# Sliding-window attention beside a gated feed-forward: small vector operations on other engines, masked maxima in two instructions, and TensorE's blocks taken from two lanes

## The chip, the cores and the metric

The kernel runs on one core of one Trainium2 chip. The metric is device time in microseconds, the median of the runs shown. Lower is better.

## What is computed

Sequence length S = 2048, model width D = 512, 32 heads of width 16, window W = 256, feed-forward width F = 1792, all float32:

```python
xn = layernorm(x)
q, k, v = heads(xn @ wqkv)
scores = (q @ k.T) / 4                      # key within the last 256 tokens, else -1e9
s = (softmax(scores) @ v) @ wo
h = silu(xn @ w1) * (xn @ w3)
g = silu(h @ w2)
return x + s * g
```

## The kernel before

**Number format.** Each float32 operand of a large matmul is cut into a float16 high half and a float16 low half, after a scaling by a power of two, and three products (high by high, high by low, low by high) stand for one. So every weight tile passes through a chain: a scale that is worked out from sums of squares (`powers`, `measure`, `measure_down`, a dozen VectorE instructions on 1 to 6 columns), a scaled copy and a rounding on ScalarE (L319, L320), a subtraction in two halves on GpSimd (L316). During the first quarter of the tokens these cut weights are used straight away and stored to DRAM; later quarters load them back.

**Stages.** The tokens are worked in four tiles of 512, t = 0 to 3. Heads go in four groups g of eight, each group in two parts p, which makes 32 units (t, g, p). Beside the units run the projections (L550, L520), the gate and up matmuls of the feed-forward for 14 blocks f (`gate_up`, L937), the down projection (`down`, L987, for t = 0 and the end; `product`, L1040, with a seven-product scheme for halves after that) and the output projection (`total`, L1118).

**Attention.** `pass1` computes scores of a row of queries (L604) only to find each query's maximum. Two 512-column banks hold the scores, one per head r. For each bank one VectorE instruction adds a mask (`MW` or `M1`, 0 or -1e30) and takes the maximum (L616), followed by a read of the accumulator. At the end of a unit the maxima are scaled and cut into two float16 parts on VectorE (L621, L622, tile `NM`), turned by a small matmul (L631), copied out (L637) and sent by DMA to two extra rows of the queries, so that `pass2`'s score matmuls (L678) subtract them. `pass2` adds masks to some blocks (L685, VectorE), takes the exponential (L688, ScalarE) and multiplies by V (L706). Each V head has a 17th column of ones, whose sums are the softmax denominators; `normalise` inverts them (L743) and scales them by `sc["o"]` (L744). K's extra rows hold +4096 and the maxima go in with a minus sign.

**Tokens prepared beside.** For t = 1 to 3, `prepare` computes mean and variance (L422, L423), then a reciprocal square root by a bit trick and three Newton steps on [128, 4] tiles, all on VectorE (`rstd`, L427 to L437), centres the tokens (L440) and turns them through unused columns of score banks (`turn_beside`, L478), where VectorE writes the float16 high part (L487) and the rest (L488).

**Banks.** Dense matmuls (tile size 128x128) accumulate in two PSUM banks m0 and m1 in turn. Scores use two tiles s of two banks and one tile po. A down block in bank m1 is added to its SBUF sum by VectorE (L1007) before the next block may use m1.

**What sets the order.** TensorE executes in the order in which the program is written: `spread` distributes dense pieces between five batches of score matmuls per unit. For VectorE, ScalarE, GpSimd and the DMA queue on SyncE, `listed` plays the program through a cost model (`arrange`) and puts each engine's instructions in the order in which they are taken there, by latest start; three rounds, the best is kept.

Of the kernel before, what the change touches and what calls it, by code (L numbers as in the profile page):

```python
# [21 lines left out]
P = 128  # L22
# [26 lines left out]
TWO_ONES = struct.unpack("f", struct.pack("ee", ONE, ONE))[0]  # L49
# [44 lines left out]
def tile_block(ctx: ExitStack, tc: tile.TileContext, x, wqkv, wo, w1, w3, w2, out):  # L94
# [121 lines left out]

    MK = const.tile([P, 3, 2, 64], BF16, name="MK")
# [48 lines left out]
    def powers(sb, n, p2, inv, s=None):  # L266
# [16 lines left out]
        def rest():  # L283
            if s is None:
                nc.vector.tensor_scalar(al, ps, 2.08, 1e-30, op0=ALU.mult, op1=ALU.max)
            else:
                with urgent():
                    nc.vector.tensor_scalar(al, s[:, 0, WIN:WIN + n], 2.08, 1e-30, op0=ALU.mult, op1=ALU.max)
                    nc.vector.scalar_tensor_tensor(al, s[:, 1, WIN:WIN + n], 2.08, al, op0=ALU.mult, op1=ALU.add)

            nc.vector.tensor_scalar(al.bitcast(I32), al.bitcast(I32), 24, 23, op0=ALU.logical_shift_right,
                                    op1=ALU.logical_shift_left)
            nc.vector.tensor_scalar(p2, al, 2.0**63, None, op0=ALU.mult)
            nc.vector.reciprocal(inv, p2)
# [8 lines left out]

    def scaled(a, by, name):
        t = const.tile([P, 1], F32, name=name)
        nc.vector.tensor_scalar(t, a, by, None, op0=ALU.mult)
# [60 lines left out]
    def weights_qk(g):  # L367
# [19 lines left out]
        def cut(ks=(1, 0)):  # L387
# [12 lines left out]
            nc.vector.tensor_scalar(es, cell["p2"], cell["p2"], DH**-0.5 / QS**2, op0=ALU.mult, op1=ALU.mult)  # L400
# [9 lines left out]
    def prepare(t):  # L410
# [9 lines left out]
        def stats(b):  # L420
            st = lnpool.tile([P, nc.vector.BN_STATS_DIM], F32, name="st")
            nc.vector.bn_stats(st, xts[b])  # L422
            nc.vector.bn_aggr(mv[:, b, :], st)  # L423

# [42 lines left out]
        def turn_beside(b, n, s):  # L467
# [24 lines left out]
        return load, stats, rstd, centre, turn if t == 0 else turn_beside  # L492
# [95 lines left out]
    def pass1(t, g, p):  # L588
# [6 lines left out]
        def part(ii, a, beside):  # L595
# [17 lines left out]
            for r in range(2):  # L613
                junk = ppool.tile([P, D], BF16, name="junk", bufs=1)
                with urgent():
                    nc.vector.tensor_tensor_reduce(  # L616
                        out=junk[:, :n], in0=s[:, r, :n], in1=mask, scale=1.0,
                        scalar=NEG, op0=ALU.add, op1=ALU.max, accum_out=M[:, r, a, ii:ii + 1])
# [117 lines left out]
    def normalise(t, g):  # L736
# [33 lines left out]
    def load(t, f):  # L770
        if t:
            WF[t, f] = a, b = [take(F16) for _ in range(2)], None if halved(t, f) else take(F16)
            for k in range(2):
                nc.sync.dma_start(a[k], dW1[f, k])
            if b is not None:
                nc.sync.dma_start(b, dW2[f])
            return
        RAW[f] = raw = [take(F32) for _ in range(2)]
        for k, w in enumerate((w1, w3)):
            nc.sync.dma_start(raw[k].rearrange("p (c f) -> p c f", f=P),  # L780
                              w[:, f * P:(f + 1) * P].rearrange("(c p) f -> p c f", p=P))

    measured = set()

    def measure(f, apart=0):
# [10 lines left out]
        def rest(pp, pi):  # L796
            ff = slice(f, f + 2)
            nc.vector.tensor_scalar(pi, pi, WS, None, op0=ALU.mult)
            nc.vector.tensor_scalar(sg_scale[:, ff], pp[:, 0, :], 0.5 / (WS * XS), None, op0=ALU.mult)
            nc.vector.tensor_mul(p13[:, ff], pp[:, 0, :], pp[:, 1, :])  # L800
# [29 lines left out]
    def measure_down(k, f):  # L830
# [16 lines left out]
        def rest(p2):  # L847
            assert measured >= set(range(f0, f1))
            nc.vector.tensor_mul(p2, p2, p13[:, f0:f1])
            q = small.tile([P, 1], F32, name="q")  # L850
            nc.vector.tensor_reduce(q, p2, axis=AX.X, op=ALU.max)
            nc.vector.tensor_scalar(down_scale[:, k:k + 1], q, 1.0 / (HS * WS), None, op0=ALU.mult)
            nc.vector.reciprocal(q, q)
            sw = small.tile([P, 6], F32, name="sw2")
            nc.vector.tensor_scalar(sw[:, 0:n], p13[:, f0:f1], q, WS, op0=ALU.mult, op1=ALU.mult)
# [304 lines left out]
    def feed_forward():  # L1160
# [7 lines left out]
        for t in range(NT):  # L1168
            for f in range(FB):
# [12 lines left out]
                else:  # L1182
                    if f == 0:
                        pieces += [(0, lambda t=t, f=f: load(t, f)) for f in range(2)]
                    if f + 2 < FB:
                        pieces.append((0, lambda t=t, f=f + 2: load(t, f)))
                if f == FB - 4 and t + 2 < NT:
# [111 lines left out]
    for b in range(4):  # L1299
# [4 lines left out]
                         AF.Copy, scale=ONE)  # L1304
# [398 lines left out]
```

## Time and profile before

| | |
|---|---|
| time, median of 3 runs | 819.23 us (818.41 to 819.41) |
| the profiled execution, its own time | 821.13 us |
| span of the profiled execution | 819.3 us, mean granted TensorE clock 0.994 |
| TensorE busy | 797.9 us (97%) |
| VectorE, ScalarE, GpSimd busy | 639.2, 435.3, 358.7 us (78%, 53%, 44%) |
| DMA | 121.99 MB, mean 149 GB/s |

TensorE is the engine that the span is made of. The profile counts a matmul of 512 columns as busy for 0.38 us, to its modelled end, though the next one starts 0.22 us after it; so the 97% hides waits of up to some 0.16 us, and what a wait costs is read from the rows of the waits and the timeline. "Sparse" below means matmuls on tiles smaller than 128x128 (scores, V, turning), "dense" the others.

### The profile page before, as it was taken

Reading aid. Unit: us, or ns where it says so; the run is one execution under the profiler, and the core shown is the slowest. Engines: PE = TensorE matmul, PEld = TensorE weight load, DVE = VectorE, ACT = ScalarE, POOL = GpSimd, SP = SyncE. Lnnn points to the kernel's source line nnn. Section 1 sums busy time; section 2 is a strip of 40 time slices with the busy share of each in tenths; the row PEclk is TensorE's granted clock in tenths of the full one; section 3 lists DMA queues with packets and bytes.
Section 4 is the critical chain, followed back from the end, with each engine's and each line's share of the span. In section 5 each row is a group of like instructions: output and inputs, shape, how many; then the busy total and the mean of one; then the engine's idle time right before and its main releaser. Section 6 shows DMA issues by size and latency. Waiting matters only on the chain.

```text
span 819.3 us, 23768 instructions
## 1 busy us (share of the span) xinstructions
PE 797.9 (97%) x9088; PEld 415.8 (51%) x9088; DVE 639.2 (78%) x2044; ACT 435.3 (53%) x659; POOL 358.7 (44%) x556
## 2 busy tenths in 40 slices
PE   8999999699999999999999999999999999999998
PEld 4444444344544554454555555545555555545654
DVE  8898889977897777799778866777878787774535
ACT  6898799555636554443443455534443446544421
POOL 2247646672806433523341752514141456435252
PEclk9999999899999999999999999999999999999999
DMA  9996575268665334545364452426375543224521
GB/s 284 284 296 185 164 215 169 75 197 204 176 179 136 117 103 121 152 144 154 106 189 133 125 142 69 140 72 172 112 185 152 159 146 113 56 90 149 172 65 55
DMA packets 112835, 121.99 MB, mean 149 GB/s; under 512 B 18448, under 2 KB 77008, under 8 KB 112720
## 3 DMA queue, kind: packets, MB, share of 16 engines
q1 hardware_dynamic: 112432, 119.94, 51.2%
q8 instruction: 71, 1.16, 0.6%
q10 hardware_dynamic: 288, 0.52, 0.2%
q14 instruction: 44, 0.36, 0.1%
HBM read 83.76 MB, written 32.37 MB: 142 GB/s over the span
## 4 chain that ended last, share of the span: by engine, by line
PE 83%; DVE 12%; issue 2%; DMA 1%; ACT 1%; DVEq 0%; SPq 0%; ACTq 0%
PE m L937 32%; PE m L1040 9%; PE m L550 9%; PE po L706 8%; PE s L678 5%; PE m L1118 5%; PE m L520 5%; PE m L987 4%; DVE junk L616 3%; PE s L604 3%; DVE s L685 2%; PE po L604 2%; DVE st L422 1%; DMA qa<-dQ 1%; DVE slot L957 1%
## 5 line engine op out<-in xcount | busy, mean ns | idle before, releaser
L688 ACT ACTIVATE pt<-s,es 128x1024 f32<-128x1024 f32 x152 | 167.7, 1113 | 198.0 <-DVE s L685 193.3
L937 PE MATMUL m<-XH,slot 128*128 128x512 f16 x896 | 267.4, 380 | 1.0 <-DVE slot L952 0.8
L316 POOL TENSOR_TENSOR slot<-slot,slot 128x256 f16<-128x256 f32 (+1 forms) x222 | 148.6, 696 | 152.4 <-ACT slot L320 66.6
L937 PEld LDWEIGHTS <-slot 128*128 128x128 f16 x1344 | 124.5, 98 | 152.6 <-issue 12.3
L937 PE MATMUL m<-XL,slot 128*128 128x512 f16 x448 | 169.8, 379 | 0.0
L685 DVE TENSOR_TENSOR s<-s,MK 128x256 f32<-128x256 f32 (+2 forms) x280 | 120.7, 437 | 50.4 <-PE s L678 41.9
L616 DVE CUSTOM_DVE_ANT_0 junk<-s,MW 128x320 bf16<-128x320 f32 x276 | 134.5, 487 | 28.0 <-PE s L604 18.6
L906 POOL TENSOR_TENSOR slot<-slot,slot 128x256 f16<-128x256 f32 x133 | 87.9, 685 | 46.4 <-ACT slot L902 46.3
L1040 PE MATMUL m<-slot,slot 128*128 128x256 f16 x798 | 96.4, 276 | 2.0 <-DVE s L685 1.8
L616 DVE CUSTOM_DVE_ANT_0 junk<-po,MW 128x320 bf16<-128x320 f32 x172 | 84.0, 488 | 10.0
L1040 PEld LDWEIGHTS <-slot 128*128 128x128 f16 x798 | 76.9, 99 | 20.4 <-issue 4.5
L706 PE MATMUL po<-pt,V 64*32 64x320 f32 (+4 forms) x2880 | 78.2, 345 | 0.0
L706 PEld LDWEIGHTS po<-pt,V 64*32 64x32 f32 x2880 | 51.9, 106 | 23.8 <-PE s L604 4.0
L910 POOL TENSOR_TENSOR slot<-slot,slot 128x256 f32<-128x256 f32 x19 | 14.2, 747 | 102.8 <-DVE slot L957 96.5
L678 PE MATMUL s<-qa,KA 50*64 50x320 f16 (+3 forms) x1472 | 58.2, 259 | 1.0 <-ACT pt L688 1.0
L987 PE MATMUL m<-slot,slot 128*128 128x512 f16 x216 | 51.6, 386 | 7.0 <-DVE slot L1007 4.7
L952 DVE SCALAR_TENSOR_TENSOR slot<-slot,m 128x512 f32<-128x512 f32 x56 | 38.3, 683 | 24.0 <-ACT slot L948 23.8
L678 PEld LDWEIGHTS <-KA 50*64 50x64 f16 x1472 | 30.2, 105 | 50.9 <-issue 36.3
L716 ACT COPY os<-po 128x512 f32<-128x512 f32 x32 | 18.7, 585 | 70.2 <-PE po L706 70.2
L948 ACT ACTIVATE slot<-m,sgs 128x512 f32<-128x512 f32 x56 | 38.3, 684 | 32.2 <-PE m L937 31.3
L957 DVE SCALAR_TENSOR_TENSOR slot<-m,slot 128x512 f32<-128x512 f32 x56 | 38.5, 687 | 15.9 <-PE m L937 15.5
L604 PE MATMUL s<-KA,qa 48*64 48x320 f16 (+2 forms) x648 | 45.5, 295 | 1.9 <-DVE M L616 0.7
(170 smaller groups left out, 1137.1 us busy)
## 6 DMA issues: line engine op xcount, KB each, us to landing
slot<-dW SPq DMA_DIRECT2D x88, 256.0 KB
slot<-dR SPq DMA_DIRECT2D x56, 256.0 KB
slot<-in_B_w_dram SPq DMA_DIRECT2D x42, 256.0 KB
dW<-slot SPq DMA_DIRECT2D x32, 256.0 KB
slot<-in_A_x_dram SPq DMA_DIRECT2D x30, 256.0 KB
KA<-dK SPq DMA_DIRECT2D x24, 288.0 KB
dR<-slot SPq DMA_DIRECT2D x49, 128.0 KB
qa<-dQ SPq DMA_DIRECT2D x32, 192.0 KB
```

The costliest lines, as they stand in the source:

```text
L316: op(out[:, c], a[:, c], b[:, c])
L550: nc.tensor.matmul(cell["pp"], a[:, k, c, :], b[:, c, :], start=(c, i) == parts[0][0], stop=(c, i) == parts[-1][-1])
L604: nc.tensor.matmul(s[64 * c:64 * c + 64, r, :n], qa[rows, 2 * p + a, ii * P + 64 * c:ii * P + 64 * c + 64], ka[rows, 2 * p + a, e - n:e], ...
L616: nc.vector.tensor_tensor_reduce(out=junk[:, :n], in0=s[:, r, :n], in1=mask, scale=1.0, scalar=NEG, op0=ALU.add, op1=ALU.max, accum_out=M[ ...
L678: nc.tensor.matmul(s[64 * h:64 * h + 64, r, o:o + 64 * n], ka[rows, 2 * p + a, 64 * (m + 4):64 * (m + 5)], qa[rows, 2 * p + a, 64 * (m + k ...
L685: nc.vector.tensor_add(v, v, MK[:, kind, of:of + n, :].unsqueeze(1).to_broadcast([P, 2 * len(which), n, 64]))
L688: nc.scalar.activation(pt, s, AF.Exp, scale=es)
L706: nc.tensor.matmul(cell["po"][32 * i:32 * i + 32, h, 64 * (m + k):64 * (m + k + n)], V[64 * h:64 * h + 64, (4 * t + m // 2) % VB, hd * VW: ...
L906: nc.gpsimd.tensor_sub(made[:, D + c.start:D + c.stop], raw[:, c], made[:, c])
L937: nc.tensor.matmul(cell[k], w[:, (a * NC + c) * P:(a * NC + c + 1) * P], b[:, c, :], start=c == 0 and i == 0, stop=c == NC - 1 and i == 2)
L987: nc.tensor.matmul(ps, hh[:, a * TW + b * P:a * TW + (b + 1) * P], w[:, c * D:(c + 1) * D], start=f == f0 and i == 0, stop=f == f1 - 1 and ...
L1040: nc.tensor.matmul(ps[:, blk, :], l[:, a * D + q:a * D + q + 128], r[:, 256 * c:256 * c + 256], start=f == f0 and x == 0, stop=f == f1 - 2 ...
```

## The change

1. **Masked maxima.** For all rows but the first two of the sequence, the two mask-and-maximum instructions become one predicated copy over both banks, which puts columns 0 to 63 over columns 256 to 319 where the far mask `PM` is set, and one plain maximum over columns 64 to 319 of both banks. Nothing then masks columns that stand in the future by adding: a column inside the window takes their place, and the leading 64 columns are left out of the maximum.
2. **Small operations moved.** The two-part cut of the maxima goes to ScalarE (two instructions) and GpSimd (one). The scale chains of weights (`powers`, `measure`, `measure_down`, `scaled`, `es`, `us`) that run beside the units go to GpSimd but for their reads of PSUM, integer shifts, one maximum and one reciprocal; a reciprocal of a power of two becomes integer arithmetic. The reciprocal square root of t = 1 to 3 goes to GpSimd (`rstd_beside`, 15 instructions). The high part of turned tokens (L487) goes to ScalarE. The scaling L744 goes away: V's columns of ones hold the scale instead, written by one ScalarE instruction in place of ten GpSimd memsets. K's extra rows hold -4096.
3. **Two lanes.** TensorE's instructions are cut into blocks, dense ones of at most six matmuls and sparse ones by PSUM tile. The planner may take the head of the other lane when the next block is not ready within 300 ns, and the order it finds is kept for TensorE too.
4. **The cost model** of `arrange` has new figures, a delay for same-engine reads, a lock between GpSimd and some VectorE instructions, and four rounds.

```diff
+    def aside():
+        return nc.gpsimd if started else nc.vector
...
+            op = nc.vector if s is None else nc.gpsimd
...
+            op.tensor_scalar(p2, al, 2.0**63, None, op0=ALU.mult)
+            if s is None:
+                nc.vector.reciprocal(inv, p2)
+            else:
+                op.tensor_scalar(inv.bitcast(I32), p2.bitcast(I32), -1.0, float(254 << 23), op0=ALU.mult, op1=ALU.add)
...
+        def rstd_beside(b0, b1):
+            op = nc.gpsimd
+            ve = lnpool.tile([P, b1 - b0], F32, name="ve")
+            op.tensor_scalar(ve, mv[:, b0:b1, 1], 1e-5, None, op0=ALU.add)
...
+            for i in range(3):
+                op.tensor_mul(sq, r0, r0)
+                op.tensor_mul(sq, sq, ve)
+                op.tensor_scalar(sq, sq, -0.5, 1.5, op0=ALU.mult, op1=ALU.add)
+                op.tensor_mul(r0, r0, sq)
...
-                    nc.vector.tensor_copy(hi, pt)
+                    nc.scalar.copy(hi, pt)
                     nc.vector.tensor_sub(lo, pt, hi)
...
-            for r in range(2):
-                junk = ppool.tile([P, D], BF16, name="junk", bufs=1)
+            if i >= 2:
                 with urgent():
-                    nc.vector.tensor_tensor_reduce(
-                        out=junk[:, :n], in0=s[:, r, :n], in1=mask, scale=1.0,
-                        scalar=NEG, op0=ALU.add, op1=ALU.max, accum_out=M[:, r, a, ii:ii + 1])
+                    nc.vector.copy_predicated(s[:, :, 256:320], PM.unsqueeze(1).to_broadcast([P, 2, 64]), s[:, :, 0:64])
+                    nc.vector.tensor_reduce(M[:, :, a, ii:ii + 1], s[:, :, 64:320], axis=AX.X, op=ALU.max)
...
-                nc.vector.tensor_scalar(nm[:, 0, :], Mf, -1.0 / ONE, None, op0=ALU.mult)
-                nc.vector.scalar_tensor_tensor(nm[:, 1, :], Mf, -1.0 / ONE, nm[:, 0, :], op0=ALU.mult, op1=ALU.subtract)
+                nc.scalar.activation(Mf, Mf, AF.Copy, scale=1.0 / ONE)
+                nc.scalar.copy(nm[:, 0, :], Mf)
+                nc.gpsimd.tensor_sub(nm[:, 1, :], Mf, nm[:, 0, :])
...
-            nc.vector.tensor_scalar(dr, dr, sc["o"], None, op0=ALU.mult)
...
+PIECE, GAIN, LEADING, FOLLOW = 6, 300, 8000, 0.0
...
+            first = met[able[0]] if not open_[able[0]] else None
+            if len(able) > 1 and (first is None or first > f + GAIN):
+                o = able[1]
+                if not open_[o] and when_of[o] - when_of[able[0]] < LEADING and (
+                        first is None or max(f, met[o]) + GAIN < first):
+                    return max(f, met[o]), o
...
-    for e in engines[1:]:
+    for e in engines:
         for a, b in zip(best_order[e], best_order[e][1:]):
```

**How the orders differ.** Line numbers shift: L316 is L333 after, L604 L635, L616 L652, L646 (predicated copy) and L647 (maximum), L678 L715, L685 L722, L987 L1030, L1007 L1050, L488 L519, L440 L471.

VectorE, in the down projection of t = 0, group of blocks f = 4 to 9: bank m1 holds the sum `m_2573` (after: `m_2540`) of the first 128 tokens, and L1007 (after: L1050) empties it. Before, it stands behind the whole reciprocal square root of the next tokens:

```order
L435 SCALAR_TENSOR_TENSOR sq<-sq,ve 128x4
L436 SCALAR_TENSOR_TENSOR r_2849<-sq,r_2849 128x4
L434 TENSOR_TENSOR sq<-r_2849 128x4
L435 SCALAR_TENSOR_TENSOR sq<-sq,ve 128x4
L436 SCALAR_TENSOR_TENSOR r_2849<-sq,r_2849 128x4
L437 TENSOR_SCALAR rs<-r_2849 128x4
L440 TENSOR_SCALAR slot_2469<-slot_2469,mv,rs 128x512
L440 TENSOR_SCALAR slot_2471<-slot_2471,mv,rs 128x512
L1007 SCALAR_TENSOR_TENSOR slot_1423<-m_2573,dsc,slot_1423 128x512
L440 TENSOR_SCALAR slot_2473<-slot_2473,mv,rs 128x512
```

The same place on VectorE after the change:

```order
L722 TENSOR_TENSOR s<-s,MK 128x2x64
L646 COPY_PREDICATED s<-PM,s 128x2x64
L646 COPY_PREDICATED po<-PM,po 128x2x64
L647 TENSOR_REDUCE M<-s 128x2
L647 TENSOR_REDUCE M<-po 128x2
L519 TENSOR_TENSOR XL<-po,XH 128x2x128
L519 TENSOR_TENSOR XL<-s,XH 128x2x128
L1050 SCALAR_TENSOR_TENSOR slot_1403<-m_2540,dsc,slot_1403 128x512
L439 BN_STATS st<-slot_2440 128x6
L439 BN_STATS st<-slot_2442 128x6
```

The square root is gone from this queue, and the emptying of m1 stands behind the maxima of one score burst and behind two L519, which read what ScalarE writes.

TensorE, a few rows earlier, in the sum for the same bank; the second operand of a row is the cut w2 tile. Before, the block f = 7 is followed at once by f = 8:

```order
L987 MATMUL m_2573<-slot_2428,slot_2072 128x512
L987 LDWEIGHTS slot_2072
L987 MATMUL m_2573<-slot_2428,slot_2072 128x512
L987 LDWEIGHTS slot_2267
L987 MATMUL m_2573<-slot_2459,slot_2267 128x512
L987 LDWEIGHTS slot_2267
L987 MATMUL m_2573<-slot_2459,slot_2267 128x512
```

After the change a burst of score matmuls (L715) stands between them:

```order
L1030 MATMUL m_2540<-slot_2395,slot_2046 128x512
L1030 LDWEIGHTS slot_2046
L1030 MATMUL m_2540<-slot_2395,slot_2046 128x512
L715 LDWEIGHTS KA_149
L715 MATMUL s<-qa,KA_149 64x320
L715 LDWEIGHTS KA_149
L715 MATMUL s<-qa,KA_149 64x320
```

So the burst moved 12 dense matmuls forward, past the blocks f = 8 and 9 and the first two of the next sum. In all, 190 of TensorE's 7,456 matmul instructions changed their place relative to the order of writing, in ten such swaps; the number of dense runs between bursts goes from 165 to 170.

More of the change, by code (lines that the diff above doesn't have):

```diff
@@ L1485, in arrange @@
     before = [set() for _ in made]
+    reads = set()
     uses, last, first, n_of = {}, {}, {}, {}
@@ L1509, in arrange @@
                     (w or write) and meets(b, o) or psum and i.engine == made[j].engine != ENGINE.PE))
+                if not write:
+                    reads.update((j, k) for j, w, o in mine if w and j != k and made[j].engine == i.engine and meets(b, o))
                 mine.append((k, write, b))
@@ L1525, in cost @@
         if kind == "InstDMACopy":
-            return 420
+            return 340
+        psum, inputs, scales = False, 0, 0
+        for a in list(i.ins) + list(i.outs):
+            ap = getattr(a, "bass_ap", None)
+            if ap is not None:
+                c = 1
+                for _, m in a.ap[1:]:
+                    c *= m
+                n = max(n, c)
+                psum |= getattr(ap.tensor, "space", None) == PSUM
         for a in i.ins:
@@ L1552, in arrange @@
             after[j].append(k)
-    last = None
-    for k, i in enumerate(made):
-        if i.engine == ENGINE.PE:
-            if last is not None and tuple(i.tile_size) != last:
-                took[k] += 160
-            last = tuple(i.tile_size)
     def deadlines(nominal):
@@ L1601, in listed @@
         flying = []
-        pipe = 0.0
-        tensor = [k for k, i in enumerate(made) if i.engine == ENGINE.PE]
-        at = 0
+        pipe = port = 0.0
+        open_ = list(outside)
+        met = [0.0] * len(blocks)
+        heads = [0, 0]
+        now, at, last = None, 0, None
+        taken = []
         mine = {e: sorted((k for k, i in enumerate(made) if i.engine == e), key=lambda k: ready_then[k]) if ready_then else [] for e in engines}
```

213 lines of the change are left out of this document (160 added, 53 removed).

## The prediction

> **What bounds the kernel now.** I read the page first. TensorE is busy nearly all the time:
>
> ```profile
> PE 797.9 (97%) x9088; PEld 415.8 (51%) x9088; DVE 639.2 (78%) x2044; ACT 435.3 (53%) x659; POOL 358.7 (44%) x556
> ```
>
> So the question is not how much VectorE work goes away, but where TensorE stands still and who makes it wait. The table by stretches tells where; columns are busy us of PE, PEld, DVE, ACT, POOL, then the granted clock:
>
> ```profile
> 20.00:140.00 120.00, 116.65 (x1086) 54.15 (x1087) 104.70 (x402) 106.70 (x206) 60.82 (x93) 1.00 0.75 221
> 140.00:150.00 10.00, 7.99 (x110) 3.70 (x101) 9.41 (x31) 9.48 (x17) 9.77 (x16) 1.00 0.42 116
> 150.00:160.00 10.00, 4.97 (x40) 2.19 (x46) 9.62 (x27) 2.58 (x6) 3.88 (x7) 0.70 0.25 79
> 160.00:740.00 580.00, 577.98 (x7088) 306.01 (x7081) 459.42 (x1451) 280.12 (x382) 247.09 (x365) 1.00 0.48 136
> 740.00:760.00 20.00, 18.20 (x203) 10.42 (x188) 10.68 (x25) 9.04 (x12) 8.63 (x14) 0.91 0.54 163
> ```
>
> From 160 to 740 us PE idles 2.0 us in 580: there a lighter VectorE has nothing to give. The idle time sits in the first tile of tokens (3.4 + 2.0 + 5.0 us up to 160) and at 740 to 760 (1.8). The view of PE's waits names who ended them:
>
> ```profile
> PE m L987 <- DVE slot L1007: 4.7, 1, 4.7
> PE m L987 <- POOL slot L316: 2.0, 5, 0.6
> PE m L1040 <- DVE s L685: 1.8, 1, 1.8
> ...
> PE s L678 <- ACT pt L688: 1.0, 1, 1.0
> PE m L937 <- DVE slot L952: 0.8, 2, 0.5
> PE m L520 <- DVE slot L563: 0.8, 1, 0.8
> PE s L604 <- DVE M L616: 0.7, 1, 0.7
> ```
>
> One wait, at L987, is the largest. The timeline of PE there:
>
> ```profile
> 149.74 1.46 PE L987 MATMUL m<-slot,slot 128*128 128x512 f16 x6
> 155.85 2.72 PE L987 MATMUL m<-slot,slot 128*128 128x512 f16 x6 [4.66 <-DVE slot L1007]
> 158.94 0.48 PE L604 MATMUL s<-KA,qa 48*64 48x320 f16 x4 [0.37 <-ACT pt L688]
> ```
>
> and VectorE's in the same microseconds:
>
> ```profile
> 147.38 0.38 DVE L427 TENSOR_SCALAR ve<-mv 128x4 f32<-128x4 f32 x1
> ...
> 153.30 0.59 DVE L436 SCALAR_TENSOR_TENSOR r<-sq,r 128x4 f32<-128x4 f32 x1
> 153.93 0.17 DVE L437 TENSOR_SCALAR rs<-r 128x4 f32<-128x4 f32 x1
> 154.14 1.00 DVE L440 TENSOR_SCALAR slot<-slot,mv,rs 128x512 f32<-128x512 f32 x2
> 155.05 0.75 DVE L1007 SCALAR_TENSOR_TENSOR slot<-m,dsc,slot 128x512 f32<-128x512 f32 x1
> ```
>
> VectorE spends 147.4 to 155.0 on the reciprocal square root of later tokens, four columns wide, and on centring. L1007, which empties bank m1, stands behind it in VectorE's queue, and TensorE stands behind L1007.
>
> **The change, part by part.**
>
> *The square root leaves VectorE.* The wait of 4.66 us goes. With it goes a slow clock: six matmuls took 1.46 us before the wait and 2.72 after it, 1.26 more, and a granted clock of 0.70 over ten microseconds is at most 3.0; I take 2.0, as the slow stretch goes on past the six matmuls. The 0.37 at 158.94 goes too, since VectorE would reach the scores earlier. Sum: 4.66 + 2.0 + 0.37 = 7.0. What is late next? In VectorE's new order L1050 stands behind one burst's work: two masks, which stay as they are,
>
> ```profile
> L685 DVE TENSOR_TENSOR s<-s,MK 128x256 f32<-128x256 f32 (+2 forms) x280 | 120.7, 437 | 50.4 <-PE s L678 41.9
> ```
>
> two predicated copies (0.27) and two maxima (0.66, both estimated below), and two L519, taken as long as the 0.42 of L487 below. With L1050's own 0.75 this is 2 x (0.44 + 0.27 + 0.66 + 0.42) + 0.75 = 4.3 us, an estimate. Between that burst and the next use of m1 stand 24 dense matmuls at 0.22, or 5.3 us. So VectorE is in time by about 1 us, if ScalarE is, and no wait takes the old one's place in the sum.
>
> *Other VectorE-ended waits.* L678 (1.0, whose L688 waited for a mask behind the square root's tail and a centring), L937 0.8, L520 0.8, L604 0.7: 3.3 us. I take 2.5, for a lighter queue shortens but does not abolish them; ends 0 and 3.3.
>
> *Maxima.* Per pair of banks before: two L616 and two accumulator reads.
>
> ```profile
> L616 DVE CUSTOM_DVE_ANT_0 junk<-s,MW 128x320 bf16<-128x320 f32 x276 | 134.5, 487 | 28.0 <-PE s L604 18.6 <-PE s L478 1.6
> ```
> ```profile
> L616 DVE DVE_READ_ACCUMULATOR2_ANT M<- 128x1 f32 x512 | 42.4, 83 | 0.0
> ```
>
> That is 2 x (0.487 + 0.083) = 1.14 us. After, the trace has no such instruction; nearest are 128 columns read from PSUM for the copy and 512 columns from PSUM for the maximum:
>
> ```profile
> L637 DVE CAST mt<-s 32x128 f16<-32x128 f32 x32 | 8.7, 273 | 0.0
> ```
> ```profile
> L719 DVE TENSOR_TENSOR os<-os,po 128x512 f32<-128x512 f32 (+1 forms) x32 | 21.2, 663 | 7.2 <-ACT os L716 7.2
> ```
>
> 0.27 + 0.66 = 0.94. The copy may cost up to an L616 (0.49), then 1.15. For the 224 pairs in the program VectorE gains 46 us or loses 2. I take the gain, as L637 is of the copy's size. On the time it is worth nothing of its own: from 160 to 740 VectorE works 459 us of 580 and PE hardly waits, and the first tile's part is in the 2.5 above.
>
> *ScalarE gets more.* Before 150 us it is busy 106.70 + 9.48 of 130. The casts and cuts that move there, in that stretch (VectorE us, count):
>
> ```profile
> 20.00:150.00 130.00, 1.68 (x4) 1.00 0.73 213
> ```
> ```profile
> 20.00:150.00 130.00, 1.52 (x5) 1.00 0.73 213
> ```
>
> The first row is L487, the second L621. Four casts of 0.42; ten short instructions, between the accumulator read and the smallest cast that the trace has:
>
> ```profile
> L247 ACT ACTIVATION_READ_ACCUMULATOR sqa<-slot 128x1 f32 x34 | 6.4, 189 | 0.0
> ```
> ```profile
> 307.73 0.39 ACT L902 CAST slot<-slot 128x256 f16<-128x256 f32 x1
> ```
>
> so 1.7 + 10 x 0.25 + 0.4 for V's ones = 4.6 us, against 13.8 idle. I let 1.0 of it reach TensorE; ends 0 and 4.6.
>
> *GpSimd gets more.* Eleven small instructions stand between the preceding cuts and the last w2 tile at 130 to 146 us, where GpSimd is busy 9.77 of 10 and L987 waits for it. Nearest rows:
>
> ```profile
> L1318 POOL MEMSET V<- 128x32 f32 x10 | 0.9, 150 | 0.0
> ```
> ```profile
> L316 POOL TENSOR_TENSOR slot<-slot,slot 128x256 f16<-128x256 f32 (+1 forms) x222 | 148.6, 696 | 152.4 <-ACT slot L320 66.6
> ```
>
> At 0.15 to 0.30 each they are 1.7 to 3.3 us. Against them, the burst moved ahead of f = 8 fills the wait, of which the list has 2.0. I take 0; ends -2.0 and +3.3. The Trainium skill speaks against this part: "GPSIMD Engine Reference", section 4.1, prefers VectorE for elementwise work, with GpSimd about twice as slow. The trace agrees for long tiles (696 ns for 256 columns against 420 for L487's 256). By that rule alone the 0.17 us of L437 would be 0.34 on GpSimd, eleven of them 3.7 us, and the predicted time up to 815.3.
>
> *Lanes.* Ten swaps among 7,456 matmuls; five more bursts, each a step into small tiles and a step back:
>
> ```profile
> 303.40 0.38 PE L937 MATMUL m<-XL,slot 128*128 128x512 f16 x1
> 303.71 0.41 PE L678 MATMUL s<-qa,KA 50*64 50x320 f16 x8
> 303.95 0.31 PE L604 MATMUL s<-KA,qa 48*64 48x320 f16 x4
> 304.09 0.30 PE L604 MATMUL po<-KA,qa 48*64 48x320 f16 x4
> 304.32 0.61 PE L937 MATMUL m<-XH,slot 128*128 128x512 f16 x2
> ```
>
> Into it: 0.31 instead of 0.22; out of it: 0.23 after L604 instead of 0.14. So 0.18 a burst, 0.9 for five.
>
> *740 to 760.* The row of waits above names a mask for L1040, but PE's weight loads, which go ahead of the matmuls, waited for a transfer:
>
> ```profile
> PEld L1040 <- DMA slot<-dR: 2.1, 1, 2.1
> ```
>
> The first dR tile of a product set is asked for after the output tile whose slot it takes has been written; that chain of stores and loads is the same after, so 1.8 us and a clock of 0.91 (1.8 more) stay: 0 in the sum, -3.6 if a shift dissolves it.
>
> *No cost:* the new masks, the sign of 4096 and V's ones; they are hidden behind the loads at the start. L744 and the moved reciprocals are in the lighter queue.
>
> Sum on the profiled span: 819.3 - 7.0 - 2.5 + 1.0 + 0 + 0.9 = 811.7. This execution's own time is 821.13, 1.83 above its span and 1.9 above the median of 819.23; so 811.7 + 1.83 - 1.9 = **811.6**.
>
> **Rivals.**
> - *Better, 806.0:* the GpSimd wait (2.0) and the dR wait with its clock (3.6) go as well: 811.6 - 5.6. All of VectorE's 3.3 and no cost of ScalarE and bursts would be 2.7 less, 803.3. For it: the moved burst stands right at the GpSimd wait, and an earlier VectorE lets the output tile be stored earlier. Against it: the dR chain has the same links.
> - *No change, 818.6:* the place at 150 us stays. L1050 is behind two L519, which wait for ScalarE's casts, and these stand among weight cuts of 0.6 to 0.7 us. If ScalarE is 6 us late there (the margin of 1 and the old wait of 4.7), all 7.0 come back. Against it: ScalarE was busy 2.58 of 10 after 150.
> - *Slower, 823.6:* the new hop at all 24 turnings. Cast and rest followed each other on VectorE; now the rest waits for a ScalarE cast that can stand behind an exponential of 1.11 us, with the score bank held and VectorE's queue behind it. At 0.5 us each that is 12 us. It decides from (819.2 - 811.6) / 24 = 0.32 us a turning. For it: only three score tiles exist. Against it: ScalarE is busy 280 of 580 us later, and bursts are some 5 us apart.
> - *The lanes fill every wait behind VectorE and GpSimd:* this would be the 803.3 above. The order speaks against it: of the ten swaps one lies at L987's waits, and none at 740 to 760.
>
> The first rival counts the clock at 740 to 760 together with the wait, since the row has 1.8 us of idle TensorE and a clock of 0.91 in the same window. The Trainium skill ("TensorE: Matmul & The Clock Gate", Part 1) lets the clock fall after an idle window of about 3.4 us. By that rule a wait of 1.8 us would not slow the clock, the place would be worth 1.8 and the rival 807.8; the trace does not agree with the threshold, as it shows the fall after a shorter wait.
>
> **Numbers.** Forecast 0.52 (own range 806 to 817, with GpSimd's +3.3 and a clock loss), better 0.12, no change 0.13, slower 0.18, other costs that I don't see 0.05. A change of 0.2%, 1.6 us, is about what a measurement of this kernel can tell. Faster: 0.52 + 0.12 + 0.02 of the third case = 0.66; the same 0.11; slower 0.23. The range from 803.5 to 823 leaves out little below and most of the slower case above.
>
> **What would show it.** In the profile after: no wait of L1030 for VectorE above 1 us, a clock of 1.00 at 140 to 160; GpSimd waits of L1030 within 0 to 4 us; the pair of maxima at 0.9 to 1.2 us; VectorE busy 70 to 95 us less; PE idle from 160 to 740 still about 2 us; the wait at some 745 us still there. I am wrong if score matmuls wait for L519 or for ScalarE's casts, or if a new slow stretch of the clock shows.

## The result

| | before | after |
|---|---|---|
| median, 6 runs each | 819.6 us (818.41 to 821.44) | **813.69 us** (811.84 to 815.83) |
| ratio after to before | | 0.9923, 95% interval 0.9908 to 0.9938 |
| span of the profiled execution | 819.3 us | 811.8 us |

The change makes the kernel 6 us (0.8%) faster. The forecast was 811.6. The head of the page after:

```profile
PE 796.1 (98%) x9088; PEld 415.6 (51%) x9088; DVE 578.5 (71%) x1400; ACT 449.9 (55%) x748; POOL 383.0 (47%) x680
```

VectorE lost 60.7 us of work, TensorE's span 7.5. The table by stretches (columns as before):

```profile
0.00:20.00 20.00, 15.56 (x69) 7.56 (x70) 15.91 (x55) 12.77 (x24) 5.28 (x25) 0.91 0.99 315
140.00:150.00 10.00, 8.76 (x119) 4.48 (x117) 8.99 (x28) 9.00 (x17) 9.85 (x16) 1.00 0.40 119
150.00:160.00 10.00, 10.00 (x155) 5.21 (x154) 5.03 (x15) 6.08 (x12) 9.26 (x25) 1.00 0.15 45
160.00:740.00 580.00, 578.02 (x7080) 306.14 (x7078) 427.45 (x949) 295.31 (x455) 263.33 (x431) 1.00 0.51 140
740.00:760.00 20.00, 17.91 (x214) 11.40 (x214) 7.35 (x16) 6.25 (x8) 3.92 (x6) 0.83 0.51 149
```

and PE's waits:

```profile
PE m L487 <- DVE slot L471: 3.2, 1, 3.2
PE m L1083 <- DMA slot<-dR: 3.2, 1, 3.2
PE s L715 <- ACT pt L725: 1.7, 2, 1.0
...
PE s L635 <- ACT pt L725: 1.0, 1, 1.0
PE m L1030 <- POOL slot L333: 0.8, 3, 0.3
```

The wait at the down projection is gone, and 150 to 160 us is full at clock 1.00. Two places got worse: the start (a new wait of 3.2 us for the centring; the clock over the first 20 us is 0.91, before 1.00) and 740 us (the dR wait is 3.2 instead of 1.8, the clock 0.83 instead of 0.91).

**A ledger.** The tables don't show what a stretch is worth, since stretches hold different work in the two runs. So I matched every matmul of one profile with the same matmul of the other, by the order in which the program writes them, and took the difference of their start times. What the difference grows by is what a place lost. The boundaries are at 15, 132, 161, 734 and 758 us of the kernel before; all numbers are us against before's profile, and minus is a gain:

| kernel | start | to 132 | 132-161 | 161-734 | 734-758 | rest | span |
|---|---|---|---|---|---|---|---|
| after | +2.4 | -2.6 | -7.0 | -3.0 | +2.6 | 0.0 | -7.5 |
| b_sqrt | -0.5 | +1.9 | -7.6 | +3.7 | +0.4 | +0.4 | -1.7 |
| maxima_back | -0.3 | -0.3 | -3.8 | +3.8 | +0.7 | 0.0 | 0.0 |
| lanes_off | +1.2 | -0.1 | -6.3 | +0.4 | +3.2 | 0.0 | -1.6 |
| give_last | +1.1 | -0.6 | -6.1 | -1.8 | -3.5 | +1.2 | -9.7 |
| hb_sqrt | +0.1 | +2.2 | -0.4 | -0.4 | -1.7 | 0.0 | -0.2 |
| hb_maxima | 0.0 | -1.8 | 0.0 | -1.6 | +0.1 | 0.0 | -3.3 |
| held_sqrt | +2.3 | -1.0 | -7.0 | -2.0 | +1.1 | 0.0 | -6.5 |
| held_both | +3.8 | -1.6 | -7.0 | -3.0 | +4.7 | 0.0 | -3.1 |
| b_plan | +2.5 | -0.2 | -8.3 | +3.2 | -0.6 | +4.6 | +1.2 |
| held_lanes | +1.5 | -1.8 | -4.7 | -4.0 | +0.9 | 0.0 | -8.0 |
| held_fix | +0.3 | -0.5 | -7.0 | -3.0 | -2.1 | 0.0 | -12.3 |
| held_cast | +2.2 | -2.6 | -9.1 | -4.0 | +1.0 | 0.0 | -12.5 |

One profile against one profile carries some scatter. After, held_sqrt and held_cast have the same queues at the start and at 740 us; they differ by 0.2 at the one and by up to 1.6 at the other. And before's profiled execution is 1.5 us above its median of 819.6, so the ledger overstates a gain by about that. Verdicts are read from the timed medians; the ledger says where.

### The profile page after: what moved, and what is told of

It is laid out like the page before. It is cut to its first block, busy times and chain, and to the rows that moved or that the text cites. A ratio compares the mean times of both kernels' runs of the same rounds, so it can differ in the third digit from the quotient of the medians.

```text
span 811.8 us, 23266 instructions
## 1 busy us (share of the span) xinstructions
PE 796.1 (98%) x9088; PEld 415.6 (51%) x9088; DVE 578.5 (71%) x1400; ACT 449.9 (55%) x748; POOL 383.0 (47%) x680
## 4 chain that ended last, share of the span: by engine, by line
PE 83%; issue 4%; DMA 4%; ACT 3%; POOL 2%; SPq 2%; DVE 2%; ACTq 0%; POOLq 0%; DVEq 0%
PE m L980 31%; PE m L1083 11%; PE po L743 9%; PE m L581 8%; PE s L715 5%; PE m L1030 5%; PE m L1161 5%; PE m L551 3%; PE s L635 3%; POOL slot L333 2%; PE po L635 1%; DMA slot<-dW 1%; DMA slot<-in_B_w_dram 1%; SPq L786 1%; DMA dm<-mt 1%
## 5 line engine op out<-in xcount | busy, mean ns | idle before, releaser
L333 POOL TENSOR_TENSOR slot<-slot,slot 128x256 f16<-128x256 f32 (+1 forms) x222 | 148.8, 695 | 123.1 <-ACT slot L337 44.8
L722 DVE TENSOR_TENSOR s<-s,MK 128x256 f32<-128x256 f32 (+2 forms) x280 | 121.3, 437 | 71.6 <-PE s L715 61.2
L647 DVE TENSOR_REDUCE M<-s 128x2 f32<-128x512 f32 x138 | 94.9, 690 | 3.1
L647 DVE TENSOR_REDUCE M<-po 128x2 f32<-128x512 f32 x86 | 59.2, 689 | 1.6
L715 PE MATMUL s<-qa,KA 50*64 50x320 f16 (+3 forms) x1472 | 58.4, 259 | 1.7 <-ACT pt L725 1.7
L715 PEld LDWEIGHTS <-KA 50*64 50x64 f16 x1472 | 30.3, 105 | 51.8 <-issue 46.1
L646 DVE COPY_PREDICATED s<-PM,s 128x128 f32<-128x128 uint8 x138 | 39.2, 287 | 23.9 <-PE s L635 20.0
L1030 PE MATMUL m<-slot,slot 128*128 128x512 f16 x216 | 49.7, 380 | 1.0 <-POOL slot L333 0.8
L659 POOL TENSOR_TENSOR NM<-M,NM 128x16 f16<-128x16 f32 x32 | 7.1, 221 | 84.3 <-ACT NM L658 65.2
L635 PE MATMUL s<-KA,qa 48*64 48x320 f16 (+2 forms) x648 | 45.6, 294 | 1.1 <-ACT pt L725 1.0
```

The source lines that it names most:

```text
L333: op(out[:, c], a[:, c], b[:, c])
L635: nc.tensor.matmul(s[64 * c:64 * c + 64, r, :n], qa[rows, 2 * p + a, ii * P + 64 * c:ii * P + 64 * c + 64], ka[rows, 2 * p + a, e - n:e], ...
L647: nc.vector.tensor_reduce(M[:, :, a, ii:ii + 1], s[:, :, 64:320], axis=AX.X, op=ALU.max)
L715: nc.tensor.matmul(s[64 * h:64 * h + 64, r, o:o + 64 * n], ka[rows, 2 * p + a, 64 * (m + 4):64 * (m + 5)], qa[rows, 2 * p + a, 64 * (m + k ...
L722: nc.vector.tensor_add(v, v, MK[:, kind, of:of + n, :].unsqueeze(1).to_broadcast([P, 2 * len(which), n, 64]))
L1030: nc.tensor.matmul(ps, hh[:, a * TW + b * P:a * TW + (b + 1) * P], w[:, c * D:(c + 1) * D], start=f == f0 and i == 0, stop=f == f1 - 1 and ...
```

## The experiments

Three parts of the change were undone or done alone, and one line that bears on the wait at 740 us was changed (give_last), with the planner free to plan anew:

```diff
b_sqrt (on before)       +  return load, stats, rstd if t == 0 else rstd_beside, centre, ...
maxima_back (on after)   -  if i >= 2:
                         +  if i >= 99:
lanes_off (on after)     -  PIECE, GAIN, LEADING, FOLLOW = 6, 300, 8000, 0.0
                         +  PIECE, GAIN, LEADING, FOLLOW = 6, 300, 0, 0.0
give_last (on after)     -  give(made, *done, xr, after=6)
                         +  give(*done, xr, made, after=6)
```

> The kernel before, with the reciprocal square root of t = 1 to 3 alone moved to GpSimd (15 instructions). Theory (the forecast's first term): the wait of 4.7 us for L1007 and the slow clock behind it go, so this part alone gives 6 to 7.4 us: 812 to 813.5 us, with no wait of L987 for VectorE above 1 us and a clock of 1.00 at 150 to 160 us. Rival 1 (the chain only changes its place: the centring and L1007 now wait for GpSimd, which is busy with weight cuts at 140 to 150): 0 to 3 us, 816 to 820, and a wait of L987 for VectorE or GpSimd of 2 us or more at 145 to 160. Rival 2 (the gain needs the lighter maxima in front of L1007 as well): 3 us, 816.

820.58 us, ratio 1.0007 (0.9997 to 1.0018). The place at 150 us gives its 7.6, and the kernel is no faster: 1.9 are lost before it and 3.7 after it, net of gains, in many steps of 0.3 to 1.0 us, most of them far from any square root.

> The kernel after, with the two mask-and-maximum instructions for every row of scores, as before. Forecast: the maxima have no time of their own in 160 to 740 us, so 0 to 1 us slower than after (813.7 to 814.7). Rival (from the two traces side by side: some fourteen steps of 0.2 to 0.3 us, nearly all at score matmuls L635 into the bank po, sum 2.7 us between 160 and 740): the longer pair holds the bank po longer, and those steps come back: 2.5 to 4 us slower than after, 816 to 818, with TensorE's dense matmuls as fast and the steps back at L635.

821.85 us, 1.0036 (1.0023 to 1.0048): 8 us slower than after by the medians (9 by the two ratios), twice the rival's bound. But 132 to 161 us changed too, with a new wait of 2.7 us of scores for a scale of weights on VectorE (L301), so this run does not price the maxima alone.

> The kernel after, with LEADING = 0, so that the planner never takes the other lane and TensorE runs in the order of writing. Forecast: the ten swaps cost 0.9 and may save up to 2 us at the down projection of t = 0: between 1 us faster and 1.5 us slower than after (812.7 to 815.2). Rival (the lanes are what removed the wait at 150 us, by moving a burst of scores ahead of two blocks): 4 us slower or more, 818 and up, with a wait of L1030 of 2 us or more at 140 to 155 us.

818.01 us, 0.9976 (0.9965 to 0.9987): 4 us slower than after. The time is the rival's, but TensorE has no wait at 150 us, where the rival put it, so neither theory fits.

> The kernel after, with one line changed: total() gives back the output tile last, behind the two tiles that were multiplied into it, so the first dR load of the product set at 740 us takes a slot that VectorE frees, not one that an output store frees. Theory (the slot chain store, then load, is the wait): the wait of 3.2 us and the 2.9 us lost to the clock behind it go or shrink to a third: 4 to 6 us faster than after, 807.5 to 809.7. Rival (the load itself is late for another reason: the queue on SyncE, or the DMA engines' own load): the wait stays at 2.5 to 3.5 us, 813 to 814.

813.29 us, 0.9919 (0.9906 to 0.9932), as fast as after. In the ledger the place gives 6.1 against after (from +2.6 to -3.5), and the new plan loses 4 elsewhere. The 2 us that remain between the two profiles are not in the timed medians, which differ by 0.4.

These four share a fault. Each edit makes the planner arrange over 10,000 instructions anew, and a new plan moves places that have nothing to do with the edit by up to 4 us either way. So the next kernels keep a plan. The program is built twice; the first pass is the unchanged kernel and yields the planned start of each instruction, the second is the changed one, whose engines take their instructions in the order of those starts ("held"; `hb_` means before's plan, `held_` after's):

```diff
+    if HELD:
+        when = HELD[0]
+        change(made, when)
+        for e in engines:
+            order = sorted((k for k, i in enumerate(made) if i.engine == e), key=lambda k: when[k])
...
+        return
```

**The square root.**

```diff
hb_sqrt     rstd_beside for t > 0, in the second pass
held_sqrt   -  op = nc.gpsimd
            +  op = nc.vector if HELD else nc.gpsimd
b_plan      tile_block of before, with arrange, streams and listed of after
```

> The kernel before with its own order kept for every engine (the planner runs on the unchanged program, and the instructions of the changed one are put at the planned times); only the square root of t = 1 to 3 is issued on GpSimd, at the times at which it stood on VectorE. Theory (re-planning hid the gain of the earlier run): with nothing else moved the 7.4 us of the place at 150 us are seen whole, 811.5 to 813 us, and every other stretch is within 1 us of before. Rival (the gain is paid back elsewhere by GpSimd or by VectorE's earlier work, whatever the order): 817 to 820, with the loss spread over 160 to 740 us again.

820.92 us, 1.0014 (1.0003 to 1.0025): no gain. The wait did not go, it changed hands. GpSimd's timeline in hb_sqrt (L316 cuts w2, L428 to L437 are the root):

```profile
148.53 0.23 POOL L428 TENSOR_SCALAR ve<-mv 128x4 f32<-128x4 f32 x1 [1.84 <-DVE mv L423]
...
149.11 0.67 POOL L316 TENSOR_TENSOR slot<-slot,slot 128x256 f16<-128x256 f32 x1
149.74 0.20 POOL L433 TENSOR_TENSOR sq<-r 128x4 f32<-128x4 f32 x1
...
151.97 0.20 POOL L433 TENSOR_TENSOR sq<-r 128x4 f32<-128x4 f32 x1
152.12 0.67 POOL L316 TENSOR_TENSOR slot<-slot,slot 128x256 f16<-128x256 f32 x1
```

and TensorE's beside it (L1001 is the down projection there):

```profile
149.83 0.38 PE L1001 MATMUL m<-slot,slot 128*128 128x512 f16 x1 [2.90 <-POOL slot L316]
152.84 3.17 PE L1001 MATMUL m<-slot,slot 128*128 128x512 f16 x7 [2.63 <-POOL slot L316]
```

The two cuts that TensorE needs stand in GpSimd's queue behind 1.84 us of waiting for the variances and behind nine small instructions. "GPSIMD Engine Reference", section 4.1, of the Trainium skill takes GpSimd to be about twice as slow as VectorE for operations with two inputs. On four columns the traces have 0.20 for the multiplication on GpSimd (L433) against 0.16 for it on VectorE (L434 in before, where nothing holds it up), so not the speed of the instructions but the queue is what costs.

The run has such a place a second time, at the root of t = 1. There VectorE's centring waits for the root on GpSimd, two masks stand behind the centring, and TensorE waits for an exponential behind the masks:

```profile
92.34 0.99 DVE L454 TENSOR_SCALAR slot<-slot,mv,rs 128x512 f32<-128x512 f32 x1 [4.81 <-POOL rs L437]
95.27 0.42 PE L692 MATMUL s<-qa,KA 50*64 50x320 f16 x10 [3.18 <-ACT pt L702]
```

Matched by start times, TensorE loses 3.9 us there, with what follows the wait. Net of gains elsewhere this is the +2.2 up to 132 us in the ledger.

The root was also long where it stood. Here are two of VectorE's rows in before, the same multiplication twice, and GpSimd's row beside the second:

```profile
148.61 0.16 DVE L434 TENSOR_TENSOR sq<-r 128x4 f32<-128x4 f32 x1
152.05 0.59 DVE L434 TENSOR_TENSOR sq<-r 128x4 f32<-128x4 f32 x1
150.70 3.17 POOL L316 TENSOR_TENSOR slot<-slot,slot 128x256 f16<-128x256 f32 x5
```

Ten of the root's thirteen instructions took 0.38 to 0.65 us there. Each of the ten ran beside a GpSimd instruction and ended within 0.03 us after the end of one. The other three, and all thirteen of the first root at the start, beside which GpSimd ran nothing, took 0.16 to 0.17. That is 4.1 us more than the ten would have taken otherwise, of a wait of 4.66. So, by an estimate from these rows, the root in the same place would have cost TensorE some 0.5 us if GpSimd had not been cutting weights beside it; no run tests this.

> The kernel after with its own order kept for every engine; only the 15 instructions of the square root of t = 1 to 3 go back to VectorE, at the times at which they stood on GpSimd. Theory (the place at 150 us is the root standing in front of L1050): a wait of L1030 for VectorE of 3 to 5 us at 145 to 156 us and a slow clock behind it, 5 to 8 us slower than after, 819 to 822. Rival (VectorE is now light enough to do both, the lighter maxima being what removed the wait): 0 to 2 us slower, 813.7 to 815.7.

814.98 us, 0.9943 (0.9930 to 0.9955): 1.6 us slower than after by the two ratios, and 132 to 161 us as good as in after. With the root on VectorE the wait stays away. VectorE's timeline after tells why:

```profile
148.11 0.41 DVE L519 TENSOR_TENSOR XL<-s,XH 128x256 f16<-128x256 f32 x1
148.44 0.74 DVE L1050 SCALAR_TENSOR_TENSOR slot<-m,dsc,slot 128x512 f32<-128x512 f32 x1
149.10 1.28 DVE L439 BATCH_NORM_STATS2 st<-slot 128x6 f32<-128x512 f32 x2
150.30 0.30 DVE L440 BATCH_NORM_AGGREGATE mv<-st 128x2 f32<-128x6 f32 x2
```

The last two of the four statistics, without which the root can't begin, now stand behind L1050; before, the root and the first centrings stood ahead of it. The rows of the order shown with the change had this (L439 right below L1050), and I read only that the root was missing above it.

> The kernel before with all its operations where they were, but with the planner of the kernel after (new cost figures, two lanes, TensorE's order kept from the plan). Theory (the place at 150 us went because the new plan puts the next tokens' statistics, root and centring behind L1007, not because of the engine of the root): the wait of 4.7 us and its slow clock go here too, 7 us or most of it in the stretch 148 to 161 us, while the steps at the score bank po stay; with the plan's scatter elsewhere 812 to 817 us. Rival (the lighter VectorE queue is needed for it): the wait of L1007 stays at 3 us or more, 818 to 822.

825.05 us, 1.0057 (1.0039 to 1.0075): slower than before. But its ledger has -8.3 at 132 to 161. Its VectorE, with every operation and the heavy maxima in place, empties m1 before the root begins, as after does:

```profile
149.34 0.42 DVE L487 CAST XH<-po 128x256 f16<-128x256 f32 x1
149.68 0.74 DVE L1007 SCALAR_TENSOR_TENSOR slot<-m,dsc,slot 128x512 f32<-128x512 f32 x1
...
158.12 0.19 DVE L427 TENSOR_SCALAR ve<-mv 128x4 f32<-128x4 f32 x1
```

So the gain of this place does not come from the engine that does the root; it comes with the plan. The plan has two parts here. One is where it puts the next tokens' preparation on VectorE. The other is the burst that TensorE takes forward past the blocks f = 8 and 9, which b_plan has at this place too. Taking the swaps back (held_lanes, below) leaves 4.7 of the 7.0, so the first part is worth some 4.7 and the second 2.3. No run moves the preparation alone in before's order; that it is the cause of the 4.7 is read from the rows. The new planner alone loses more elsewhere than the place gives: 3.2 from 161 to 734, 2.5 at the start and 4.6 at the end.

**The maxima.**

```diff
hb_maxima   -  for r in range(2): ... nc.vector.tensor_tensor_reduce(...)
            +  nc.vector.copy_predicated(s[:, :, 256:320], PM..., s[:, :, 0:64])
            +  nc.vector.tensor_reduce(M[:, :, a, ii:ii + 1], s[:, :, 64:320], axis=AX.X, op=ALU.max)
```

> The kernel before with its own order kept for every engine; only each pair of masked maxima (rows after the first two) is replaced by the predicated copy and the plain maximum, in the same two places of VectorE's queue. Forecast: no time of its own from 160 to 740 us, 0.2 us at most there, and up to 2.5 us in the first tile of tokens: 817 to 819.5 us. Rival (the score bank po comes free 0.2 us earlier each time, which shows as steps at L604 and L706): 2.5 to 4 us less from 160 to 740 us, and 813.5 to 816 us in all.

814.38 us, 0.9940 (0.9925 to 0.9956): 5 us faster than before, with nothing else moved but the making of the new mask at the start. This is the rival's time, and the forecast of no time of its own is wrong. The profile accounts for 3.3 of it; its execution was the longest of the six (817.85 us) and had a mean clock of 0.994, the other five 0.995 to 0.998, so the rest is likely a slow stretch that they don't have; no profile of theirs shows it. One of the places, before, VectorE and then TensorE (tile `po` is one bank of scores):

```profile
262.75 0.49 DVE L616 CUSTOM_DVE_ANT_0 junk<-po,MW 128x320 bf16<-128x320 f32 x1
263.16 0.08 DVE L616 DVE_READ_ACCUMULATOR2_ANT M<- 128x1 f32 x1
263.16 0.68 DVE L952 SCALAR_TENSOR_TENSOR slot<-slot,m 128x512 f32<-128x512 f32 x1
263.76 0.48 DVE L616 CUSTOM_DVE_ANT_0 junk<-po,MW 128x320 bf16<-128x320 f32 x1
```
```profile
263.55 0.64 PE L678 MATMUL s<-qa,KA 50*64 50x320 f16 x24
264.31 0.33 PE L604 MATMUL po<-KA,qa 48*64 48x320 f16 x4
```

and the same scores after:

```profile
255.59 0.68 DVE L647 TENSOR_REDUCE M<-po 128x2 f32<-128x512 f32 x1
```
```profile
256.57 0.64 PE L715 MATMUL s<-qa,KA 50*64 50x320 f16 x24
257.04 0.31 PE L635 MATMUL po<-KA,qa 48*64 48x320 f16 x4
```

The next scores for `po` start 0.76 us after L678 before and 0.47 after L715 now, since the old ones are read earlier; in hb_maxima, where the order around them is that of before, it is 0.49. TensorE is marked busy throughout, because the modelled end of the matmul ahead covers the gap: no row of waits shows these 0.3 us. From 161 to 734 us hb_maxima has some ten such steps of 0.2 to 0.5 us, and a few smaller losses against them.

**The hop to ScalarE.**

```diff
held_cast   -  nc.scalar.copy(hi, pt)
            +  (nc.vector.tensor_copy if HELD else nc.scalar.copy)(hi, pt)
```

> The kernel after with its own order kept; only the rounding of turned tokens (24 instructions) goes back from ScalarE to VectorE, right ahead of the rest that reads it. The rival slower than before priced this hop at up to 0.5 us at each of 24 turnings; by that, taking it back gives 4 to 12 us, 802 to 810. Theory (VectorE waits about 0.35 us for ScalarE at each, 8.3 us in all by the groups, but TensorE does not wait for VectorE there): within 1 us of after, 812.7 to 814.7.

809.32 us, 0.9872 (0.9853 to 0.9890), 4.2 us faster than after by the two ratios. "VectorE waits, TensorE doesn't" was wrong. VectorE did wait for most casts, 17 of 24:

```profile
L519 DVE TENSOR_TENSOR XL<-s,XH 128x256 f16<-128x256 f32 x15 | 6.3, 422 | 3.5 <-ACT XH L518 3.5
L519 DVE TENSOR_TENSOR XL<-po,XH 128x256 f16<-128x256 f32 x9 | 3.8, 422 | 4.8 <-ACT XH L518 4.8
```

TensorE waited too, not for the cast but for an exponential that stands behind one in ScalarE's queue, and the cast itself waits there for TensorE to turn the tokens. After, ScalarE and TensorE:

```profile
132.25 0.37 ACT L518 CAST XH<-s 128x256 f16<-128x256 f32 x1 [1.55 <-PE m L980]
...
133.66 1.10 ACT L725 ACTIVATE pt<-s,es 128x1024 f32<-128x1024 f32 x1
```
```profile
133.40 0.41 PE L715 MATMUL s<-qa,KA 50*64 50x320 f16 x10
134.82 0.25 PE L635 MATMUL s<-KA,qa 48*64 48x128 f16 x4 [1.01 <-ACT pt L725]
```

and the same place in held_cast:

```profile
130.79 1.11 ACT L725 ACTIVATE pt<-s,es 128x1024 f32<-128x1024 f32 x1
```
```profile
133.15 0.41 PE L715 MATMUL s<-qa,KA 50*64 50x320 f16 x10
133.39 0.23 PE L635 MATMUL s<-KA,qa 48*64 48x128 f16 x4
```

The waits of score matmuls for exponentials (L715 and L635), 2.7 us in after, are 0.2 in held_cast. By the ledger 2.1 us come at 132 to 161 and 1.0 from 161 to 734; the 1.6 at 740 are the scatter named above.

**Lanes, and the two places that got worse.**

```diff
held_lanes   key=lambda k: k if e == ENGINE.PE else when[k]
held_both    give(*done, xr, made) at (t, b) = (2, 1); root, scale's cast and centring in one go
held_fix     the same; VectorE's and ScalarE's start as in before; on SyncE the first dR load
             goes ahead of the output store, the one that needs the store's slot goes behind it
```

> The kernel after with its own order kept for VectorE, ScalarE, GpSimd and SyncE; TensorE alone goes back to the order of writing. Forecast: five bursts less, 0.9 us faster, and up to 2 us slower at the w2 cuts at 140 to 146 us: 812.8 to 815.7. Rival (read from the run without lanes, where the stretch up to 148 us and the one from 160 to 734 us were 3.2 and 3.4 us slower than after): the swaps carry 3 us or more, 816.7 to 820, with waits of TensorE at the ten places.

813.11 us, 0.9914 (0.9898 to 0.9931): the intervals of this kernel and of after overlap, so the ten swaps are worth nothing that can be measured. They pay 2.3 us at 132 to 161, where without them L1030 waits 2.9 us for GpSimd's w2 cuts instead of 0.8, and cost as much or a little more elsewhere.

> The kernel after with its own order kept but at two places: at the start VectorE does the first square root and the centring in one go, ahead of the first weights' scale, with the first ScalarE cast of tokens ahead of the first rounded weight; and at 740 us the first dR loads take the slots that VectorE frees, the output tile's slot going to the second load. Theory: 1.5 to 2.5 us at the start and 4 to 6 us at 740, 805 to 808 us, with no wait of L1083 for DMA above 1 us. Rival (each place has a second wait right behind the first): 810 to 813.

819.19 us, 0.9992 (0.9983 to 1.0001): the theory is out, and the time is worse than even the rival's. With the queues kept, the load that now needs the output tile's slot stands right behind the store, and SyncE's queue stands with it: 6.1 us of waiting for dR. At the start the cast that was brought forward was the only one; three stayed behind the sums of squares of the weights (L256) in ScalarE's queue.

> The kernel after with its own order kept, and both places mended with the queues: at the start VectorE and ScalarE work in the order that the kernel before has up to the fourth cut of tokens; at 740 us the first dR load takes the slot that VectorE frees and stands ahead of the output store in SyncE's queue, the load that needs the output tile's slot stands behind it. Theory: 2 to 2.5 us at the start and 5 to 6 us at 740 us, 805.2 to 807 us. Rival (a second wait right behind each, as in the run with the slots alone): 810 to 815.

808.97 us, 0.9862 (0.9845 to 0.9878): 5 us faster than after by the two ratios, between the ranges of the theory and of the rival. Of PE's waits the dR row shrinks and the centring's nearly goes:

```profile
PE m L581 <- ACT whi L327: 1.5, 1, 1.5
PE m L1083 <- DMA slot<-dR: 1.3, 2, 0.9
...
PE m L487 <- DVE slot L471: 0.4, 1, 0.4
```

The 2.1 us won at the start are paid back, most of them at 22 us, at L581, whose cut weights now stand behind the casts of tokens; the 4.7 us at 740 stay. held_cast and held_fix each beat both kernels by more than their intervals. They mend different places; the two together were not run.

## Why the prediction was right, and where it was not

The total was right (7.6 us forecast on the span, 7.5 in the profile), the terms were not. Errors of both signs cancelled, so that the two numbers agree this closely is luck.

- *Square root, -7.0:* the place gave 7.0, with clock and all. The reason given, that the root leaves VectorE, fell: hb_sqrt has the root on GpSimd and the wait, held_sqrt and b_plan have it on VectorE and no wait. It was the place in VectorE's queue, beside GpSimd's cuts, and for 2.3 of the 7.0 the moved burst. The step that failed is taking the rows that are missing ahead of L1050 for the cause, where what counts is what stands behind it now.
- *Maxima, no time of their own:* the pair took 0.287 + 0.690 = 0.98 us (forecast 0.94), but alone it is worth 5 us. The step "from 160 to 740 PE hardly waits" took the 2.0 us of idle TensorE for all there is to gain. The whole change gave 3.0 there, the maxima alone 1.6 (and 1.8 before 132 us), while TensorE's idle time after stayed at 2.0. The page's busy time hides gaps below the modelled tail of a matmul.
- *Other VectorE-ended waits, -2.5:* -2.6 from 15 to 132 us, of which the maxima alone give 1.8.
- *ScalarE, +1.0 (ends 0 and 4.6):* the casts alone cost about 4.2 us, near the upper end. So the slower rival's mechanism was there; at 0.18 us a turning it stayed under the 0.32 from which it decides, and it acted through the exponentials behind the casts.
- *GpSimd, 0 (-2.0 to +3.3):* L1030 waits 0.8 us for it, before 2.0. That the moved burst fills this wait was right: without the swaps it is 2.9. The small ones on four columns took 0.19 to 0.23 us each on GpSimd, not 0.34. hb_sqrt, with 5.5 us, shows what instructions like these cost in another order.
- *Lanes, +0.9:* nothing measurable in all, a gain of 2.3 at 132 to 161 and as much lost elsewhere.
- *740 to 760, 0:* +2.6. The chain was the same, as said, but not its place in SyncE's queue among the other transfers: the wait grew by 1.4 us, and the clock's loss behind it by 1.2. Three other profiles with the same queues there (held_sqrt, held_lanes, held_cast) have waits of 2.8 to 3.0 us and 0.9 to 1.1 in all, so about 1 of the 2.6 is sure. held_fix, which moves two loads in that queue, takes 4.7 back.
- *The start, "no cost":* +2.4. The new plan mixes the first weights' scale with the first root on VectorE, whose queue then stands 0.36 and 0.91 us for results of others:

```profile
8.29 0.17 DVE L268 CAST sb<-ssq 128x2 bf16<-128x2 f32 x1 [0.36 <-ACT sqa L256]
...
9.63 0.16 DVE L294 TENSOR_SCALAR al<-s 128x1 f32<-128x1 f32 x1 [0.91 <-PE s L283]
...
11.47 0.75 DVE L328 SCALAR_TENSOR_TENSOR wlo<-slot,sw,whi 128x512 f16<-128x512 f32 x1
12.14 1.91 DVE L471 TENSOR_SCALAR slot<-slot,mv,rs 128x512 f32<-128x512 f32 x4
```

VectorE's work fell by 61 us where 70 to 95 were forecast. Of the signs named for being wrong, two showed: score matmuls wait 2.7 us for exponentials behind ScalarE's casts (1.4 for exponentials before), and the start has a new slow stretch of the clock. The rival of the lanes is out; the rival in which the place at 150 us stays did not happen after, but hb_sqrt is what it would look like.

Still open: why plans that were made anew (b_sqrt, maxima_back, b_plan) lose 3 to 4 us between 161 and 734 us, which neither before nor after does; and what held_cast and held_fix give together.

## What to carry to other kernels

When a planner sets the order, test a part of a change with the plan held, since a new plan costs or gives as much as the part. Where a wait goes, ask which instruction now stands ahead of the one that was waited for, and not which one has left the engine. Moving a small operation to an idle engine puts it in a queue: look at what stands behind it there, as the exponentials behind a 0.37 us cast did here. And look at how long a short VectorE instruction takes beside a busy GpSimd before pricing it: here 0.6 us in place of 0.16.

## What the hardware showed that I had not expected

The same wait did and did not slow the clock. At the first product of the set at 740 us TensorE waited 1.79 us before, and 1.77 us in hb_sqrt. The stretch of before, quoted with the prediction, has a clock of 0.91, that of hb_sqrt 1.00, and the same 36 matmuls took 5.77 and 4.10 us. Here are the rows of before and of hb_sqrt, with hb_sqrt's stretch, and last the row of after:

```profile
750.88 5.77 PE L1040 MATMUL m<-slot,slot 128*128 128x256 f16 x36 [1.79 <-DVE s L685]
```
```profile
752.36 4.10 PE L1054 MATMUL m<-slot,slot 128*128 128x256 f16 x36 [1.77 <-DVE s L699]
740.00:760.00 20.00, 18.23 (x237) 10.62 (x237) 11.85 (x30) 9.70 (x13) 10.04 (x16) 1.00 0.54 163
```
```profile
742.09 7.01 PE L1083 MATMUL m<-slot,slot 128*128 128x256 f16 x36 [3.19 <-DMA slot<-dR]
```

The ledger has 1.7 us between before and hb_sqrt, all behind the wait. In held_sqrt and held_cast, with after's queues and waits of 2.91 and 2.83 us, the 36 matmuls took 5.77. So what a wait of this length costs beyond itself, from nothing to as much again, is not read from its length; it is one reason why two profiles of the same queues differ. The timed executions of before beside the experiments agree: those with a mean clock of 0.993 or 0.994 took 820.7 to 822.7 us, those with 0.998 took 818.2 to 820.0.
